# Row halves for the MLP, mixer and value products of a fused attention and MLP kernel

## The chip, the cores and the metric

The kernel runs on one core of a Trainium2 chip. The metric is the device time of one execution in microseconds (us). The time before is 290.8 us, the median of three runs (290.4 to 291.24). A ratio is the mean time of one kernel's fast runs over the mean time of the fast runs of the kernel before in the same rounds, so it is not quite the ratio of the medians that are quoted next to it.

Engine names in the profile: PE is TensorE's matmuls, PEld its weight loads, DVE is VectorE, ACT is ScalarE, POOL is GpSimd.

## The reference

Block-sparse attention over 4 batches, 8 heads, 768 positions and 64 features per head, then a low-rank mixer over the positions and an MLP with relu over the channels:

```python
scores = scale * q @ k.T                  # per head, 768 x 768
attn   = softmax(where(mask, scores, -1e9))
x      = attn @ v                         # heads side by side: [4, 768, 512]
h      = x.T @ U @ V                      # mixer, rank 32
u      = x + h.T
out    = u + maximum(u @ w_ch1, 0) @ w_ch2   # 512 -> 2048 -> 512
```

## The kernel before

The work streams by head pairs: 16 pairs, 4 per batch. The scores of a pair come in nine units. A unit is two or four matmuls into a tile `psc` of two PSUM banks, an exp of 1.02 us on ScalarE into an SBUF tile `est`, and a mask product on `est` of 0.83 us on VectorE. (In the first batch the mask comes in through further rows of the score matmuls, which use all 128 rows there, and there is no mask product.) Two `psc` tiles take four of the eight PSUM banks. The other four serve everything else: the value products (`pav`), the mixer's two products (`pa`, `ph`), MLP1 (`pt`) and MLP2 (`pch`). MLP work of the batch before is filled in between the scores of this batch, and ACT or DVE empties each bank: relu for `pt`, a sum with the residual for `ph` and `pch`, a normalisation for `pav`.

```python
    pscp = tile_pool(name="pscp", bufs=2, space=PSUM)   # two psc tiles, two banks each
    psp  = tile_pool(name="psp", bufs=1, space=PSUM)    # four tags: bank0 .. bank3
    ...
    def pst_tile(shape, dtype, name, tag=None):
        if tag is None:
            n = min(range(4), key=lambda n: banks[n])   # the bank that is free first
    ...
    def scores(i, u, est):
        psc = pscp.tile([P, 2, 512], FP32, tag="psc", name="psc")
        ...     # one head contracts over rows 0-63, the other over rows 64-127
                mm(o, kT[rows[h], kc], qT[rows[h], q0:q1], True, True)

    def weights(ests, g, j, h):                         # which unit a value matmul reads
        tr, kind = divmod(g, 2)
        if j < 4:
            return ests[3 * tr + kind][:, h, j * P : (j + 1) * P]
        return ests[3 * tr + 2][:, h, kind * QB + (j - 4) * P : ...]

    def values(i, c, ests, xs, xh):                     # c: three of six column tiles
        pav = new_pav()                                 # one bank
        for h in range(2):
            for j in range(3):
                for g in range(T):
                    mm(pav[:, j, h, :], weights(ests, g, 3 * c + j, h), vts[...], g == 0, g == T - 1)
        norm(i, c, pav, xs, xh)
    ...
        def w1(jj, c):                                  # MLP1: one bank, four full matmuls
            pt = pst_tile([P, HS], FP32, "pt")
            for cc in range(NCC):
                mm(pt, w1t[:, cc, ...], uT[:, cc, ...], cc == 0, cc == NCC - 1)
            # relu on ACT or DVE, whichever a small clock model says is done first
    ...
    groups += [stream[n : n + 2] for n in range(SINGLE, len(stream), 2)]   # scores: two units at a time
    ...
                for at, fn in zip((0, 1, 3), steps):    # values 0, values 1, product a
                    work.append((gi + at, fn))
                beside.append((gi + 5, steps[3]))       # product h, right behind scores
```

The softmax here doesn't subtract the row's maximum and nothing guards it: scores larger than these inputs give would overflow.

## Time and profile before

The first two lines of the page of the kernel before give the span and each engine's busy time, share of the span and instructions; the next two are its chain of waits, as shares of the span by engine and then by line.

```profile
span 288.9 us, 6744 instructions
PE 279.8 (97%) x2765; PEld 162.0 (56%) x2765; DVE 188.3 (65%) x347; ACT 178.0 (62%) x232; POOL 95.3 (33%) x126
...
PE 84%; DMA 6%; ACT 6%; issue 2%; DVE 1%; POOL 1%; SPq 0%; ACTq 0%; DVEq 0%; POOLq 0%
```

TensorE is busy 97 % of the time and 84 % of the chain is TensorE itself, so nothing else sets the pace. The windows view has one row per stretch: its length, then the busy time and count of PE, PEld, DVE, ACT and POOL, the granted clock, the DMA share and GB/s.

```profile
120.00:135.00 15.00, 15.00 (x182) 9.34 (x180) 11.54 (x21) 10.76 (x15) 6.26 (x8) 1.00 0.58 159
135.00:150.00 15.00, 15.00 (x138) 8.63 (x135) 12.97 (x24) 11.96 (x17) 5.18 (x7) 1.00 0.47 108
```

PE shows 15 of 15 us. The groups view, with shapes apart, names the four products that matter (busy us, mean ns of one, idle before). From the second batch on, the score matmuls and the mixer's product h use 64 rows; MLP1, MLP2, the values and the mixer's product a use 128.

```profile
L129 PE MATMUL pt<-uT,w1t 128*128 128x384 f16 x512 | 89.1, 327 | 0.2 <-DVE uT L564 0.2
L129 PE MATMUL pch<-w2t,tT 128*128 128x512 f16 x368 | 84.4, 380 | 0.0
L129 PE MATMUL pav<-vt,est 128*128 128x65 f16 x1152 | 46.4, 193 | 0.1
L129 PE MATMUL psc<-qT,kT 64*128 64x512 f16 x144 | 25.3, 382 | 0.5 <-ACT est L419 0.5
```

What the busy table does not show is TensorE's loss at changes between 64 and 128 rows, because a matmul record covers that time. It must be read from the distance between starts. An MLP1 matmul follows another after 163 ns (384 columns) and an MLP2 matmul another after 216 ns (512 columns), so 0.415 ns a column and about 3 ns. A score behind MLP1 starts after 258 ns instead of 163, behind MLP2 after 312 instead of 216, behind a value product after 126 instead of 32.

### The profile page before, as it was taken

The page shows a single profiled execution, that of the slowest core. Times are in us where ns is not written, and L with a number is a line of the kernel's source. Part 1 is how long each engine was busy: PE and PEld are TensorE (multiplying, and loading weights), DVE is VectorE, ACT ScalarE, POOL GpSimd, SP SyncE. Part 2 cuts the span into 40 slices and gives each one's busy share as a digit, 9 for nine tenths or more (in the row PEclk, how much of TensorE's full clock was granted, in tenths as well). Part 3 has the DMA queues.
Part 4 walks back from the last instruction along what each step waited for, and adds up shares of the span by engine and source line. Part 5 has one row for each costly group of instructions (what it writes and reads, how often), then busy time and mean ns, then how long its engine had stood idle before and what let it go on. Part 6 is the DMA issues. An engine that isn't in the chain of part 4 may idle for free.

```text
span 288.9 us, 6744 instructions
## 1 busy us (share of the span) xinstructions
PE 279.8 (97%) x2765; PEld 162.0 (56%) x2765; DVE 188.3 (65%) x347; ACT 178.0 (62%) x232; POOL 95.3 (33%) x126
## 2 busy tenths in 40 slices
PE   7979998899999999999999999999999999999996
PEld 2557775455746454556565545466564644665443
DVE  5756768689997978887886695779787622000112
ACT  3879999687785757577776555577875000776000
POOL 1549853207344454526244261603031201000000
PEclk9999999999999999999999999999999999999999
DMA  5999999962457677773444365161010225000122
GB/s 157 331 261 262 236 254 268 243 169 76 92 140 107 213 160 205 202 153 64 144 108 142 106 173 143 50 93 31 0 31 0 58 80 102 36 0 2 70 75 74
DMA packets 46414, 36.91 MB, mean 128 GB/s; under 512 B 27272, under 2 KB 42896, under 8 KB 46384
## 3 DMA queue, kind: packets, MB, share of 16 engines
q1 hardware_dynamic: 43208, 32.06, 41.6%
q0 software_dynamic: 2688, 4.19, 8.1%
q8 instruction: 21, 0.34, 0.5%
q10 hardware_dynamic: 488, 0.24, 0.3%
q14 instruction: 9, 0.07, 0.1%
HBM read 27.80 MB, written 6.29 MB: 118 GB/s over the span
## 4 chain that ended last, share of the span: by engine, by line
PE 84%; DMA 6%; ACT 6%; issue 2%; DVE 1%; POOL 1%; SPq 0%; ACTq 0%; DVEq 0%; POOLq 0%
PE pt L129 29%; PE pch L129 29%; PE psc L129 11%; PE pav L129 10%; ACT est L419 5%; DMA ka<-onehot_const 3%; DMA qld<-in_q_dram 2%; PE pa L129 2%; DMA kld<-in_k_dram 1%; PE ph L129 1%; PE pturn L194 0%; PE puT L563 0%; DVE uT L564 0%; DVE xh L453 0%; DVE m L384 0%
## 5 line engine op out<-in xcount | busy, mean ns | idle before, releaser
L419 ACT ACTIVATE est<-psc 128x1024 f16<-128x1024 f32 x144 | 138.8, 1023 | 47.4 <-PE psc L129 47.2
L129 PE MATMUL pt<-uT,w1t 128*128 128x384 f16 x512 | 89.1, 327 | 0.2 <-DVE uT L564 0.2
L129 PE MATMUL pch<-w2t,tT 128*128 128x512 f16 (+2 forms) x400 | 87.9, 371 | 0.0
L431 DVE TENSOR_TENSOR est<-est,m 128x1024 f16<-128x1024 f16 x108 | 84.7, 828 | 0.0
L129 PEld LDWEIGHTS <-w1t 128*128 128x128 f16 x512 | 47.6, 98 | 38.2 <-issue 8.4
L587 ACT ACTIVATE tT<-pt 128x384 f16<-128x384 f32 x82 | 39.3, 495 | 36.1 <-PE pt L129 34.9
L129 PEld LDWEIGHTS <-tT 128*128 128x128 f16 x400 | 36.4, 98 | 44.3 <-issue 5.4
L129 PEld LDWEIGHTS <-est 128*128 128x128 f16 x1152 | 44.0, 97 | 10.6 <-issue 0.5
L471 POOL CAST xh<-xs 128x384 f16<-128x384 f32 x30 | 21.4, 716 | 84.7 <-DVE xs L453 82.5
L608 DVE TENSOR_TENSOR of<-xf,pch 128x512 f32<-128x512 f32 (+2 forms) x25 | 16.6, 662 | 49.9 <-PE pch L129 49.8
L129 PE MATMUL pav<-vt,est 128*128 128x65 f16 x1152 | 46.4, 193 | 0.1
L129 PE MATMUL psc<-qT,kT 64*128 64x512 f16 (+1 forms) x288 | 33.9, 327 | 0.9 <-ACT est L419 0.8
L549 POOL CAST uh<-xf 128x384 f16<-128x384 f32 x24 | 16.1, 697 | 38.3 <-issue 33.6
L590 DVE TENSOR_SCALAR tT<-pt 128x384 f16<-128x384 f32 x46 | 24.2, 548 | 0.9 <-PE pt L129 0.7
L129 PE MATMUL psc<-qa,ka 128*128 128x512 f16 (+1 forms) x96 | 21.8, 326 | 1.9 <-DMA ka<-onehot_const 1.5
L448 DVE RECIPROCAL rcp<-pav 128x6 f32<-128x6 f32 x32 | 6.2, 194 | 21.1 <-PE pav L129 20.6
L453 DVE TENSOR_TENSOR xs<-pav,rcp 128x384 f32<-128x384 f32 x32 | 17.8, 557 | 1.9
L188 POOL CAST kst<-kld 128x768 f16<-128x768 f32 x15 | 16.5, 1100 | 5.5 <-PE pt L129 2.0
L188 POOL CAST qst<-qld 128x768 f16<-128x768 f32 x15 | 16.5, 1100 | 3.6 <-PE pa L129 2.5
L129 PEld LDWEIGHTS <-kT 64*128 64x128 f16 x288 | 10.1, 94 | 13.4 <-issue 8.8
L182 POOL CAST vt<-vld 128x768 f16<-128x768 f32 x16 | 15.0, 939 | 5.7 <-DMA vld<-in_v_dram 5.7
L544 DVE TENSOR_TENSOR xf<-xs,ph 128x384 f32<-128x384 f32 x24 | 12.2, 548 | 4.5 <-PE ph L129 4.5
(57 smaller groups left out, 111.5 us busy)
## 6 DMA issues: line engine op xcount, KB each, us to landing
vld<-in_v_dram SPq DMA_DIRECT2D x16, 384.0 KB, 5.0
out_dram<-of SPq DMA_DIRECT2D x23, 256.0 KB, 2.2
qld<-in_q_dram SPq DMA_DIRECT2D x15, 384.0 KB, 4.4
kld<-in_k_dram SPq DMA_DIRECT2D x15, 384.0 KB, 4.1
w1t<-in_moe_w_ch_dram POOLq DMA_DIRECT2D x4, 512.0 KB, 10.2
w2t<-in_moe_w_ch_dram POOLq DMA_DIRECT2D x4, 512.0 KB, 19.5
qld<-in_q_dram SPq DMA_DIRECT2D x1, 256.0 KB, 3.1
kld<-in_k_dram SPq DMA_DIRECT2D x1, 256.0 KB, 4.5
```

Source lines behind the costliest of these rows:

```text
L129: nc.tensor.matmul(out, lhsT, rhs, start=start, stop=stop, skip_group_check=loose)
L182: nc.gpsimd.tensor_copy(out=vts[b % 2][:, 2 * hp : 2 * hp + 2, :, 0:D], in_=ld)
L188: keep(nc.gpsimd.tensor_copy(out=st.rearrange("p t h d -> p h t d"), in_=ld))
L419: keep(nc.scalar.activation(out=est, in_=psc, func=AF.Exp, scale=0.125))
L431: keep(nc.vector.tensor_tensor(out=o, in0=o, in1=m, op=ALU.mult))
L453: nc.vector.tensor_tensor(out=o.rearrange("p j (h d) -> p j h d", h=2), in0=pav[:, :, :, 0:D], in1=rcp[:, :, :, None].broadcast_to([P, 3, ...
L471: keep(nc.gpsimd.tensor_copy(out=xh[:, 3 * c : 3 * c + 3, :], in_=x3))
L544: nc.vector.tensor_tensor(out=u3, in0=xs[:, tc3, :], in1=phs[c], op=ALU.add)
L549: keep(nc.gpsimd.tensor_copy(out=uh[:, tc3, :], in_=u3))
L587: keep(nc.scalar.activation(out=dst, in_=pt, func=AF.Relu))
L590: keep(nc.vector.tensor_scalar_max(out=dst, in0=pt, scalar1=0.0))
L608: nc.vector.tensor_add(out=of, in0=xfs[b][:, sc, n0:n1], in1=pchs[sc])
```

## The change

The intent is to do away with those changes of mode: the MLP, the mixer's product a and the value products also run as pairs of 64-row matmuls, one on rows 0 to 63 and one on rows 64 to 127, at the same time. The kernel keeps the two row halves out of each other's PSUM bank, so each step takes two banks. In its first phase the upper half adds into bank A and the lower half into bank B; then the halves swap, so that at the end each bank has the sum over all 128 rows. Before the swap TensorE waits on its own semaphore until the first phase is done. To hide that wait, the scores go in unit by unit between two phases, where the kernel before placed them two units at a time.

The diff, cut to its core:

```diff
+    def half_wait(ins):
+        nop = nc.tensor.nop(nofuse=True)
+        tc.add_manual_dep(nop.ins, ins.ins.name, ...)      # TensorE waits for its own matmul
 ...
-    def values(i, c, ests, xs, xh):
 ...
+    def values_rows(i, ests, xs, xh):
+        pavs = [new_pav(), new_pav()]
+        for phase in range(2):
+            if phase == 1:
+                half_wait(half_done(last))
+            for h in range(2):
+                for j in range(3):
+                    for g in range(T):
+                        for r in ((0, 1), (1, 0))[phase]:
+                            c = r ^ phase
+                            last = mm(pavs[c][:, j, h, :], weights(ests, g, 3 * c + j, h)[rows[r]], ...)
+        for c in range(2):
+            norm(i, c, pavs[c], xs, xh)
 ...
+    def mix_a_rows(xh, box):
+        pas = [pst_tile([P, P], FP32, "pa") for r in range(2)]   # summed on VectorE afterwards
 ...
+        def w1_rows(jj, phase):
+            if phase == 0:
+                pair[0] = [pst_tile([P, HS], FP32, "pt") for c in range(2)]
+            if phase == 1:
+                half_wait(pair[2])
+            for cc in range(NCC):
+                for r in ((0, 1), (1, 0))[phase]:
+                    c = r ^ phase
+                    last = mm(pts[c], w1t[rows[r], cc, ...], uT[rows[r], cc, ...], ...)
 ... (w2_rows likewise, two pch banks; the last batch's MLP stays on 128 rows)
-    groups = [[x] for x in stream[:SINGLE]]
-    groups += [stream[n : n + 2] for n in range(SINGLE, len(stream), 2)]
-    LATE = 8
+    groups = [[x] for x in stream]
+    LATE = 16
 ...
-                for at, fn in zip((0, 1, 3), steps):
-                    work.append((gi + at, fn))
-                beside.append((gi + 5, steps[3]))
+                work.append((gi, steps[0]))
+                work.append((gi + 5, steps[1]))
+                beside.append((gi + 9, steps[2]))
```

The mixer in row halves also needs another layout of its weights in the first batch: U is cast in four pieces instead of two, V is loaded twice, into two sets of rows that one cast covers, and one clearing of a tile falls away. From the second batch on, the transposes of q and k also take whichever bank is free first, where they had a fixed pair.

More of the change, by code (lines that the diff above doesn't have):

```diff
@@ L109, in pst_tile @@
             n = min(range(4), key=lambda n: banks[n])
+            assert banks[n] < OPEN
             clk["pe"] = max(clk["pe"], banks[n])
@@ L127, in mm, with half_done @@
         clk["pe"] += us
-        keep(
-            nc.tensor.matmul(
-                out, lhsT, rhs, start=start, stop=stop, skip_group_check=loose
-            )
-        )
+        ins = nc.tensor.matmul(
+            out, lhsT, rhs, start=start, stop=stop, skip_group_check=loose
+        )
+        keep(ins)
+        return ins
+    def half_done(ins):
+        return ins
+    def half_wait(ins):
+        nop = nc.tensor.nop(nofuse=True)
+        tc.add_manual_dep(
+            nop.ins, ins.ins.name,
+            mybir.DependencyInfo(mybir.DependencyClass.Sync, mybir.DependencyReason.DATA),
+            reason="halves",
+        )
+        keep(nop)
     id16 = consts.tile([P, P], FP16)
@@ L218 @@
     keep(nc.vector.memset(Vt, 0.0))
-    keep(nc.vector.memset(Vd, 0.0))
     qld, kld = new_ld(0, "q"), new_ld(0, "k")
@@ L357 @@
     uld = w2t[:, 3, 0 : 2 * T * R].bitcast(FP32)
-    mvld = w2t[0:R, 0:3, :].rearrange("r j d -> r (j d)").bitcast(FP32)
+    mvld = w2t[0 : 2 * R, 0:3, :].rearrange("r j d -> r (j d)").bitcast(FP32)
     def load_w1(cc):
@@ L480, in new_pav @@
         return pst_tile([P, 3, 2, D + 1], FP32, "pav", tag)
-    def values(i, c, ests, xs, xh):
+    def values_rows(i, ests, xs, xh):
         b, hp = divmod(i, HP)
-        pav = new_pav()
-        for h in range(2):
-            for j in range(3):
-                for g in range(T):
-                    mm(
-                        pav[:, j, h, :],
-                        weights(ests, g, 3 * c + j, h),
-                        vts[b % 2][:, 2 * hp + h, g, 0 : D + 1],
-                        g == 0, g == T - 1, us=0.0315,
-                    )
-        norm(i, c, pav, xs, xh)
+        pavs = [new_pav(), new_pav()]
[7 more added lines that the diff above has]
+                            c = r ^ phase
+                            last = mm(
+                                pavs[c][:, j, h, :],
+                                weights(ests, g, 3 * c + j, h)[rows[r]],
+                                vts[b % 2][rows[r], 2 * hp + h, g, 0 : D + 1],
+                                phase == 0 and h == 0 and j == 0 and g == 0,
+                                phase == 1 and g == T - 1, True, us=0.0157,
+                            )
+        for c in range(2):
+            norm(i, c, pavs[c], xs, xh)
     def mix_a(i, xh, box, part, tag=None):
@@ L504, in mix_a @@
             give_back(box["pa"], run_on("dve", 0.2))
+    def mix_a_rows(xh, box):
+        pas = [pst_tile([P, P], FP32, "pa") for r in range(2)]
+        for sc in range(T):
+            for r in range(2):
+                mm(pas[r], Ut[rows[r], sc, :], xh[rows[r], sc, :], sc == 0, sc == T - 1, us=0.027)
+        a16 = box["a"] = misc.tile([P, P], FP16, tag="a16", name="a16")
+        keep(nc.vector.tensor_copy(out=a16, in_=pas[0]))
+        give_back(pas[0], run_on("dve", 0.2))
+        keep(nc.vector.tensor_tensor(out=a16, in0=a16, in1=pas[1], op=ALU.add))
+        give_back(pas[1], run_on("dve", 0.2))
     def mix_h(i, c, a16, xs, uh, tag=None, quick=False):
@@ L583, in w1 @@
                 )
-            dst = tT[jj][:, c * HS : (c + 1) * HS]
-            ends = {e: max(clk[e], clk["pe"]) + d for e, d in (("act", 0.43), ("dve", 0.48))}
-            if ends["act"] <= ends["dve"]:
-                keep(nc.scalar.activation(out=dst, in_=pt, func=AF.Relu))
-                give_back(pt, run_on("act", 0.43))
-            else:
-                keep(nc.vector.tensor_scalar_max(out=dst, in0=pt, scalar1=0.0))
-                give_back(pt, run_on("dve", 0.48))
+            relu(tT[jj][:, c * HS : (c + 1) * HS], pt)
         pchs = {}
@@ L605, in w2 @@
             if part == 3:
-                of = opool.tile([P, n1 - n0], FP32, tag="of", name="of")
-                keep(
-                    nc.vector.tensor_add(out=of, in0=xfs[b][:, sc, n0:n1], in1=pchs[sc])
-                )
-                give_back(pchs[sc], run_on("dve", 0.6))
-                keep(
-                    nc.sync.dma_start(
-                        out=out[b].rearrange("(p t) d -> p t d", t=T)[:, sc, n0:n1],
-                        in_=of,
-                    )
-                )
+                leave(sc, n0, n1, pchs[sc])
@@ new lines, in mlp_steps, with relu @@
+        pair = {}
+        def relu(dst, pt):
+            ends = {e: max(clk[e], clk["pe"]) + d for e, d in (("act", 0.43), ("dve", 0.48))}
+            if ends["act"] <= ends["dve"]:
+                keep(nc.scalar.activation(out=dst, in_=pt, func=AF.Relu))
+                give_back(pt, run_on("act", 0.43))
+            else:
+                keep(nc.vector.tensor_scalar_max(out=dst, in0=pt, scalar1=0.0))
+                give_back(pt, run_on("dve", 0.48))
+        def w1_rows(jj, phase):
+            if phase == 0:
+                tT[jj] = tpool.tile([P, S], FP16, tag="tT", name="tT")
+                pair[0] = [pst_tile([P, HS], FP32, "pt") for c in range(2)]
+            uT = uTs[b].rearrange("p n t s -> p n (t s)")
+            pts = pair[0]
+            if phase == 1:
[3 more added lines that the diff above has]
+                    c = r ^ phase
+                    last = mm(
+                        pts[c],
+                        w1t[rows[r], cc, jj * P : (jj + 1) * P],
+                        uT[rows[r], cc, c * HS : (c + 1) * HS],
+                        phase == 0 and cc == 0, phase == 1 and cc == NCC - 1, True,
+                        us=0.081,
+                    )
+            if phase == 0:
+                pair[2] = half_done(last)
+            else:
+                for c in range(2):
+                    relu(tT[jj][:, c * HS : (c + 1) * HS], pts[c])
@@ new lines, in leave, with w2_rows @@
+        def leave(sc, n0, n1, pch):
+            of = opool.tile([P, n1 - n0], FP32, tag="of", name="of")
+            keep(nc.vector.tensor_add(out=of, in0=xfs[b][:, sc, n0:n1], in1=pch))
+            give_back(pch, run_on("dve", 0.6))
+            keep(
+                nc.sync.dma_start(
+                    out=out[b].rearrange("(p t) d -> p t d", t=T)[:, sc, n0:n1],
+                    in_=of,
+                )
+            )
+        def w2_rows(s0, phase, part):
+            if phase == 0 and part == 0:
+                pair[1] = [pst_tile([P, HD], FP32, "pch") for c in range(2)]
+            if phase == 1 and part == 0:
+                half_wait(pair[2])
+            for jj in range(4 * part, 4 * part + 4):
+                for r in ((0, 1), (1, 0))[phase]:
+                    c = r ^ phase
+                    last = mm(
+                        pair[1][c],
+                        tT[jj][rows[r], (s0 + c) * P : (s0 + c + 1) * P],
+                        w2t[rows[r], jj, :],
+                        phase == 0 and jj == 0, phase == 1 and jj == NJJ - 1, True,
+                        us=0.1085,
+                    )
+            if phase == 0 and part == 3:
+                pair[2] = half_done(last)
+            if phase == 1 and part == 3:
+                for c in range(2):
+                    leave(s0 + c, 0, HD, pair[1][c])
@@ new lines, in mlp_steps @@
+        if b < B - 1:
+            for jj in range(NJJ):
+                for phase in range(2):
+                    steps.append((0.65, lambda jj=jj, ph=phase: w1_rows(jj, ph), phase == 1))
+            for s0 in range(0, T, 2):
+                for phase in range(2):
+                    for part in range(4):
+                        steps.append(
+                            (
+                                0.87,
+                                lambda s0=s0, ph=phase, part=part: w2_rows(s0, ph, part),
+                                phase == 1 and part == 0,
+                            )
+                        )
+            return steps
@@ L618, in mlp_steps @@
         for jj in range(NJJ):
             for c in range(2):
-                steps.append((0.65, lambda jj=jj, c=c: w1(jj, c)))
+                steps.append((0.65, lambda jj=jj, c=c: w1(jj, c), False))
         for sc in range(T):
@@ L628, in mlp_steps @@
                             lambda sc=sc, part=part, n0=n0, n1=n1: w2(sc, part, n0, n1),
+                            False,
                         )
@@ L678, in turn_part @@
         if part == 0:
-            turning[nm] = pst_tile([P, T, P], FP16, "pturn", tag="ps")
+            turning[nm] = pst_tile([P, T, P], FP16, "pturn", tag="ps" if i < HP + 1 else None)
         turn_some(sts[i, nm], turning[nm], 3 * part, 3 * part + 3)
@@ L731, in at_unit @@
                 issue(2, "v")
-                keep(nc.sync.dma_start(out=mvld, in_=moe_V))
+                for h in range(2):
+                    keep(nc.sync.dma_start(out=mvld[h * R : h * R + R], in_=moe_V))
                 keep(
@@ L753, in at_unit @@
                 for h in range(2):
-                    keep(
-                        nc.gpsimd.tensor_copy(
-                            out=Ut[:, :, h * D : h * D + R],
-                            in_=uld.rearrange("p (t r) -> p t r", t=T),
+                    for r in range(2):
+                        at = h * D + r * R
+                        keep(
+                            nc.gpsimd.tensor_copy(
+                                out=Ut[rows[r], :, at : at + R],
+                                in_=uld[rows[r]].rearrange("p (t r) -> p t r", t=T),
+                            )
                         )
-                    )
                 keep(
                     nc.gpsimd.tensor_copy(
-                        out=Vt[0:R, :, :],
+                        out=Vt[0 : 2 * R, :, :],
                         in_=mvld.rearrange("r (p t) -> r t p", t=T),
@@ L767, in at_unit @@
             for h in range(2):
-                keep(nc.sync.dma_start(out=Vd[h * D : h * D + R], in_=Vt[0:R]))
+                keep(nc.sync.dma_start(out=Vd[rows[h]], in_=Vt[rows[0]]))
         if (i, u) in WLOADS:
@@ L799, in run_fill @@
         state["debt"] += us
+        n = 0
         while fill and state["debt"] > 0:
-            cost, fn = fill.popleft()
+            if fill[0][2] and n and us < 1e6:
+                break
+            cost, fn, _ = fill.popleft()
             fn()
+            n += 1
             state["debt"] -= cost
@@ L809, in pair_tail @@
         uh = xpool.tile([P, T, P], FP16, tag="uh", name="uh")
-        def both_a():
-            mix_a(i, xh, box, 0)
-            mix_a(i, xh, box, 1)
         def both_h():
@@ L819, in pair_tail @@
         return [
-            lambda: values(i, 0, ests, xs, xh),
-            lambda: values(i, 1, ests, xs, xh),
-            both_a,
+            lambda: values_rows(i, ests, xs, xh),
+            lambda: mix_a_rows(xh, box),
             both_h,
@@ L833 @@
         last = [n for n, gr in enumerate(groups) if (HP * b + HP - 1, NU - 1) in gr][0]
-        OPENS.append(last + 1 + LATE)
+        OPENS.append(last + LATE)
     for name in ("pe", "dve"):
@@ L901 @@
             to_come = [n for n in OPENS if n > gi] or [gi + 1]
-            run_fill(sum(c for c, _ in fill) / (to_come[0] - gi))
+            run_fill(sum(c for c, _, _ in fill) / (to_come[0] - gi))
         while work and work[0][0] <= gi:
```

## The prediction

> **What bounds it now.** TensorE. The busy table gives PE 97% of 288.9 us; the windows table gives PE 15.0 us of every 15 from 120 to 255 us, DVE at most 13, ACT at most 12. The chain of waits is 84% PE. The change touches the streaming stretch, about 49 to 230 us; the first batch and the last MLP stay.
>
> **What it removes.** Scores use 64 rows, all else 128: the build order counts 117 changes of mode after the first 64-row score, 13 after the change. The Trainium skill ("TensorEngine Tiling (Array Packing)", Key Properties) says that a change of mode drains TensorE. The trace agrees, in start-to-start times: score after MLP1 258 ns against 163 within MLP1, score after MLP2 312 against 216, score after values 126 against 32, MLP2 after a score 308 against 216; the first pair in a new mode takes 10 ns more. 104 changes at about 100 ns: -10.4 us.
>
> **What it does not gain.** Pairs of 64-row matmuls start 3 to 4 ns apart and repeat like one 128-row matmul: 109 ns at 256 columns, 56 at 128. I expect values near 32 ns a pair: after a wait ended, the sequencer passed 5 further instructions in 8 ns (47 ns for 7, 54 for 12), so issuing does not limit.
>
> **What it adds.**
> 1. 65 swap waits, each a semaphore wait in PE's sequencer. A matmul's update comes 340 ns after its start (384 columns; 207 at 65), and the one such wait of before that held PE let the next matmul start 136 ns after its semaphore, against 43 for a wait carried by a matmul. Estimate from these: a bare swap idles 312 ns (340+136-162), with a score unit in front about 100, with score and mixer none. The order shows 13 bare (12 within values) and 36 behind scores alone: 4.1+3.7 = +7.9 us.
> 2. Banks. Four banks serve MLP, values and mixer. Every step now takes two, and one pair stays half filled across a swap, so the next step must take the pair just finished. Before, an MLP1 eviction ended 0.70 us (median; 1.02 at p90) after its matmul, with three other banks. Walking one head pair through the new order with before's durations (exp 1.02, mask product 0.83, relu 0.5, norm 0.19+0.56 twice, mixer sum 0.55 twice): product a waits 0.35 us for relus, MLP1 after ph 0.65 for two sums, MLP1 after values 0.85 for two norms: about 1.6 us for each of seven head pairs in MLP1 stretches, 0.5 for five in MLP2; with some catching up, +8.5 us.
> 3. DVE gets 12 adds of 0.29 us, ACT 12 more relus: off the path.
>
> **Sum.** 290.8 - 10.4 + 7.9 + 8.5 = 296.8, so 297 us; 8 in 10 within 290 to 306. Chances: faster by over 2% 0.04, within 2% 0.46, slower by over 2% 0.50.
>
> **What would show it.** Right: no 90-ns steps between scores and MLP; pairs at 162 and 216 ns; some 65 semaphore waits on PE, bare ones with 0.31 us of idle; PE busy at 90 to 93% in the stretch, its idle time before pt, pa, pav naming DVE norms and sums and relus; clock 1.0. Step 2 is wrong if idle time before pt and pav stays under 3 us: then about 290. Step 1 is wrong if swaps clearly differ from 0.31 and 0.1 us.
>
> **What would make it wrong.** Value pairs slower than 32 ns (each 10 ns more is 8.6 us over 864 pairs); exps better spaced; relus falling where both engines are idle, so that banks come back in time.

## More of the kernel before

The view of PE's waits from 60 to 240 us has one line in all (who waits, for whom, us in total, times, longest).

```profile
PE psc L129 <- ACT est L419: 0.5, 1, 0.5
```

## The result

The changed kernel is correct and takes 315.65 us in the median (314.11 to 318.43, four runs), beside 290.6 us for the kernel before (290.26 to 291.24, four runs). The ratio is 1.087, with a 95 % interval of 1.079 to 1.096: slower, and outside the predicted range.

The page of the changed kernel, the lines that answer to those of before, and with them the row of TensorE's granted clock over 40 slices of the span:

```profile
span 316.6 us, 10037 instructions
PE 290.2 (92%) x4373; PEld 180.2 (57%) x4373; DVE 187.5 (59%) x346; ACT 184.8 (58%) x244; POOL 95.7 (30%) x128
...
PEclk9995999999999999999999999999999999999999
...
PE 59%; DVE 22%; ACT 6%; DMA 5%; issue 5%; POOL 1%; SPq 0%; DVEq 0%; ACTq 0%; POOLq 0%
```

VectorE does no more than before (187.5 us against 188.3), yet it now holds 22 % of the chain, against 1 %. The windows and groups of the changed kernel:

```profile
120.00:135.00 15.00, 13.74 (x260) 8.49 (x258) 11.57 (x20) 9.10 (x9) 6.34 (x8) 1.00 0.54 153
135.00:150.00 15.00, 12.74 (x266) 8.29 (x262) 11.16 (x20) 9.27 (x15) 4.73 (x7) 1.00 0.52 109
```

```profile
L129 PE MATMUL pt<-uT,w1t 64*128 64x384 f16 x768 | 78.2, 323 | 5.1 <-DVE of L674 2.1 <-DVE xs L467 1.4 <-DVE uT L598 0.4
L129 PE MATMUL pch<-w2t,tT 64*128 64x512 f16 x576 | 72.5, 376 | 1.6 <-DVE of L674 1.4
L129 PE MATMUL pav<-vt,est 64*128 64x65 f16 x1728 | 35.7, 190 | 7.0 <-DVE est L445 1.9 <-DVE xf L578 1.6 <-issue 1.1
```

The idle column has filled up: MLP1 waits for output sums (`of`) and normalisations (`xs`), the values for mixer sums (`xf`) and for the mask product (`est`). The view of PE's waits from 60 to 240 us, one line before, has ten now, of which seven are:

```profile
PE pt L129 <- DVE of L674: 2.1, 4, 1.3
PE pav L129 <- DVE est L445: 1.7, 8, 0.2
PE pav L129 <- DVE xf L578: 1.6, 6, 0.3
PE pa L129 <- DVE tT L645: 1.5, 2, 1.2
PE pt L129 <- DVE xs L467: 1.4, 4, 0.4
PE pav L129 <- issue: 1.1, 2, 0.6
PE pch L129 <- DVE of L674: 0.6, 2, 0.4
```

One value product of the changed kernel shows several losses at once. First TensorE, then VectorE, from the timeline (start us, busy us, count, idle before it and what ended that):

```profile
126.10 0.19 PE L129 MATMUL pav<-vt,est 64*128 64x65 f16 x1
126.56 0.49 PE L129 MATMUL pav<-vt,est 64*128 64x65 f16 x20 [0.28 <-DVE xf L578]
127.27 2.35 PE L129 MATMUL pav<-vt,est 64*128 64x65 f16 x116 [0.22 <-DVE est L445]
130.09 0.30 PE L129 MATMUL pav<-vt,est 64*128 64x65 f16 x7 [0.48 <-issue]
```

```profile
125.50 1.01 DVE L578 TENSOR_TENSOR xf<-xs,ph 128x384 f32<-128x384 f32 x2
126.43 0.79 DVE L445 TENSOR_TENSOR est<-est,m 128x1024 f16<-128x1024 f16 x1
```

The first half starts at 126.10 in a bank that is free. Its partner needs the other bank, in which the mixer's product h still lies: VectorE empties it until 126.51 us, and the partner starts at 126.56. Then the pair needs the last masked unit, whose mask product ends at 127.22; TensorE goes on at 127.27. In the third line a swap of 0.31 us (at 128.42) is hidden, because the records cover it. The fourth line starts after 0.48 us without any wait; point 7 below shows what it waited for.

### Where TensorE's time went

The records of matmuls cover a part of each such gap, so I counted from starts. For each row half, a matmul frees the array its columns times 0.415 ns, plus 2 ns, after its start; the time until the next start is idle, with a weight of one half for each row half. Gaps of a few ns, some 3 us in all in each kernel, are left out. Each idle time is put down to the semaphore that came last, as the build's list of waits tells it. The stretch runs from the first MLP1 matmul to the first matmul of the last batch's MLP, and is 194.4 us before and 216.8 us after (us, all from one profiled run each):

| | stretch | mode changes | swaps | banks | mask product | no wait found | other | idle in all |
|---|---|---|---|---|---|---|---|---|
| before | 194.4 | 10.4 | 0 | 0.9 | 0 | 0 | 2.6 | 13.9 |
| after | 216.8 | 0.3 | 9.2 | 20.1 | 3.8 | 2.9 | 1.5 | 37.8 |

"Banks" is every wait for an eviction: after the change mixer sums 5.9, output sums 5.4, relus 4.6, normalisations 3.4 and the mixer's copies and adds 0.8. The stretch less its idle time is 180.5 us before and 179.0 after. The columns to run are the same in both, so the 1.5 us between them is how closely the count closes, and the idle time accounts for the whole difference.

Outside the stretch the profiled run lost 5.3 us more, 4.5 of them before the first MLP1 matmul (54.5 against 50.0 us) and the rest behind the last output sum. In the first batch the mixer's first product waits 2.7 us for a cast on GpSimd that stands behind the new casts of U and V, and then the granted clock falls to half for 6.8 us, the 5 in the clock row. That costs 3.4 us at most, half of its length. The fastest run of the four (314.11 us) had a mean clock of 1.0, so the dip comes and goes.

### The profile page after: what moved, and what is told of

Its sections match the earlier page's. It is cut to its first block, busy times and chain, and to the rows that moved or that the text cites. A ratio compares the mean times of both kernels' runs of the same rounds, so it can differ in the third digit from the quotient of the medians.

```text
span 316.6 us, 10037 instructions
## 1 busy us (share of the span) xinstructions
PE 290.2 (92%) x4373; PEld 180.2 (57%) x4373; DVE 187.5 (59%) x346; ACT 184.8 (58%) x244; POOL 95.7 (30%) x128
## 4 chain that ended last, share of the span: by engine, by line
PE 59%; DVE 22%; ACT 6%; DMA 5%; issue 5%; POOL 1%; SPq 0%; DVEq 0%; ACTq 0%; POOLq 0%
PE pch L129 21%; PE pt L129 19%; DVE est L445 10%; PE pav L129 10%; ACT est L433 6%; PE psc L129 6%; DVE xf L578 3%; DMA kld<-in_k_dram 3%; DMA vld<-in_v_dram 3%; DVE xs L467 2%; DVE of L674 2%; PE pa L129 2%; DVE tT L645 1%; PE ph L129 1%; DVE rcp L462 1%
## 5 line engine op out<-in xcount | busy, mean ns | idle before, releaser
L129 PE MATMUL pt<-uT,w1t 64*128 64x384 f16 (+1 forms) x896 | 99.2, 324 | 5.1 <-DVE of L674 2.1
L129 PE MATMUL pch<-w2t,tT 64*128 64x512 f16 (+3 forms) x688 | 93.5, 372 | 1.6 <-DVE of L674 1.4
L129 PEld LDWEIGHTS <-w1t 64*128 64x128 f16 (+1 forms) x896 | 52.9, 94 | 42.7 <-issue 15.1
L129 PEld LDWEIGHTS <-tT 64*128 64x128 f16 (+1 forms) x688 | 43.7, 94 | 37.7 <-issue 5.1
L642 ACT ACTIVATE tT<-pt 128x384 f16<-128x384 f32 x94 | 44.9, 496 | 28.7 <-PE pt L129 27.3
L129 PE MATMUL pav<-vt,est 64*128 64x65 f16 (+1 forms) x2016 | 51.6, 191 | 7.1 <-DVE est L445 1.9
L129 PEld LDWEIGHTS <-est 64*128 64x128 f16 (+1 forms) x2016 | 46.0, 95 | 20.4 <-issue 11.0
L129 PE MATMUL psc<-qT,kT 64*128 64x512 f16 (+1 forms) x288 | 44.3, 323 | 0.3 <-ACT est L433 0.3
L129 PEld LDWEIGHTS <-kT 64*128 64x128 f16 x288 | 17.0, 94 | 8.9 <-issue 0.6
L645 DVE TENSOR_SCALAR tT<-pt 128x384 f16<-128x384 f32 x34 | 18.8, 553 | 5.2 <-PE pt L129 5.0
```

Source lines behind the costliest of these rows:

```text
L129: ins = nc.tensor.matmul(out, lhsT, rhs, start=start, stop=stop, skip_group_check=loose)
L642: keep(nc.scalar.activation(out=dst, in_=pt, func=AF.Relu))
L645: keep(nc.vector.tensor_scalar_max(out=dst, in0=pt, scalar1=0.0))
```

## The experiments

My theory: the loss is the pairs of banks. Every step holds two of four banks, a pair stays half filled across a swap, so the next step must take the pair that was just finished and wait for its evictions. In addition, values in row halves need the last masked unit at once. Rivals: the swaps cost more than they look; VectorE is loaded too heavily; the order of the scores does it; the first batch does it.

For all runs that follow, the table gives the same account of the stretch (us; "scores" is the scores' wait for exps):

| run | median us | ratio | stretch | mode | swaps | banks | mask | scores | no wait | other |
|---|---|---|---|---|---|---|---|---|---|---|
| after | 315.65 | 1.087 | 216.8 | 0.3 | 9.2 | 20.1 | 3.8 | 0 | 2.9 | 1.5 |
| e2_fuse | 311.96 | 1.075 | 213.6 | 0.4 | 4.2 | 21.1 | 3.8 | 0 | 2.6 | 2.0 |
| e7_late | 311.70 | 1.073 | 212.9 | 0.3 | 9.3 | 20.0 | 0.1 | 0 | 3.8 | 1.4 |
| e12_fuse_late | 310.37 | 1.068 | 212.2 | 0.4 | 4.6 | 22.5 | 0.1 | 0 | 4.0 | 1.9 |
| e8_three | 320.23 | 1.102 | 222.4 | 0.4 | 6.5 | 0.4 | 8.8 | 24.7 | 0.8 | 1.4 |
| e5_light_after | 308.97 | 1.064 | 210.2 | 0.2 | 9.2 | 16.7 | 0 | 0 | 3.9 | 1.3 |
| e3_values_full | 303.08 | 1.043 | 204.8 | 4.4 | 4.6 | 13.3 | 0.7 | 0 | 0.6 | 1.5 |
| e4_mlp_full | 314.15 | 1.081 | 216.1 | 20.6 | 3.9 | 1.4 | 6.4 | 0 | 1.1 | 2.6 |
| e9_mlp_only | 298.69 | 1.029 | 202.8 | 6.4 | 1.1 | 12.1 | 0.7 | 0 | 0.4 | 2.0 |
| e11_mlp1_only | 301.27 | 1.038 | 204.6 | 12.1 | 0.6 | 8.5 | 0.7 | 0 | 0.4 | 2.3 |
| e10_single_before | 300.82 | 1.037 | 204.6 | 20.7 | 0 | 1.1 | 0.4 | 0 | 0 | 2.0 |

The kernel before ran at 290.2 to 290.6 us in the same rounds. Each kernel was run in three rounds, four runs in all.

### The first batch's layout alone (e1_layout)

The kernel before with only the new layout of the mixer's weights:

```diff
-    keep(nc.vector.memset(Vd, 0.0))
-    keep(nc.sync.dma_start(out=mvld, in_=moe_V))
+    for h in range(2): keep(nc.sync.dma_start(out=mvld[h * R : h * R + R], in_=moe_V))
-    ... tensor_copy(out=Ut[:, :, h * D : h * D + R], in_=uld ...)
+    for r in range(2): ... tensor_copy(out=Ut[rows[r], :, at : at + R], in_=uld[rows[r]] ...)
```

> The kernel before with only the change's new first-batch layout (U copied in four row-half pieces, V loaded twice, no clearing of Vd), no row mode. Theory (a separate cost of about 4.4 us sits in the first batch, where product a waits 2.7 us for the xh cast behind the new copies on POOL, and a half clock may follow): 293 to 295 us, all of the loss before 32 us, the streaming stretch unchanged. Rival (all of the loss is in the streaming stretch): 290.6 us.

It took 293.41 us (292.74 to 293.68), ratio 1.009 (1.005 to 1.013), at full clock in the profiled run. The stretch is unchanged at 194.4 us; it starts 1.8 us later, and 1.1 us more pass behind the last output sum (3.6 us to the end against 2.5). Other runs with the new layout have 3.2 to 3.3 us there and those with the old one 2.5; why, I have not found out. So about 3 us of the change's 25 (1.4 to 3.8 by the interval of the ratio) come with the layout, in parts that the prediction took as "stays".

### The swap's wait on the next weight load (e2_fuse)

```diff
-        nop = nc.tensor.nop(nofuse=True)
+        nop = nc.tensor.nop()
```

With this the wait is not an instruction of its own, but is carried by the weight load behind it.

> The changed kernel with the swap wait put on the next weight load instead of a separate instruction of PE's sequencer (one word). Theory (swaps cost 9 us of the stretch by the accounting of its trace, bare 311 ns and 98 ns behind a score unit): each falls by 60 to 90 ns, swap idle 9.1 to about 5.5 us, time 312 us. Rival (swaps are the main loss, since each one empties PE's lead): 8 us or more fall away, below 308 us. If the swap is not bound by the sequencer at all: 315.6 us.

It took 311.96 us (310.89 to 314.96), ratio 1.075 (1.067 to 1.084). Swaps fell from 9.2 to 4.2 us in the account: a bare swap inside the values from 328 to 238 ns (mean of both halves), all swaps behind score units together from 5.2 to 1.3 us. The waits for banks stayed. Of 25 us, the swaps explain 9 and the form of their wait 5.

### Values one score unit later (e7_late)

```diff
-                work.append((gi, steps[0]))
+                work.append((gi + 1, steps[0]))
```

> The changed kernel with the value products one score unit later. Theory (values wait 3.8 us for the last mask product, since both column halves now run together right after it, and 3.9 us for the mixer sums that hold their banks): the mask wait falls below 0.5 us and the sums' wait by at least half, time 310 to 312 us. Rival (PE's waits only move to the next shared bank): 314 us or more.

It took 311.70 us (310.93 to 313.07), ratio 1.073 (1.068 to 1.078). The wait for the mask product fell from 3.8 to 0.1 us, as it must if its only cause is that the values come at once behind the last unit. The waits for banks changed places, mixer sums from 5.9 to 2.9 and normalisations from 3.4 to 5.3, and their sum stayed at 20.

### A third pair of banks (e8_three)

In the stretch the scores keep one two-bank tile, and the other serves MLP, mixer and values as a third pair:

```diff
+    def pst_pair(shape, name):
+        ...                                  # the oldest free pair of three
-        psc = pscp.tile([P, 2, 512], FP32, tag="psc", name="psc")
+        psc = psc_tile("psc")                # always the same one in the stretch
-            pts = [pst_tile([P, HS], FP32, "pt") for c in range(2)]
+            pts = pst_pair([P, HS], "pt")
```

> The changed kernel with three pairs of banks in the stretch instead of two: scores keep one two-bank buffer there, the other serves MLP, values and mixer. Theory (a step needs a whole pair and must take the one just finished, 20 us of waits for relus, norms, mixer sums and output sums): those waits fall to about 5 us, scores wait up to 4 us for exps, 301 to 306 us. Rival (DVE is too busy, evictions queue whatever the banks): waits stay above 15 us and 313 us or more.

It took 320.23 us (320.08 to 321.16), ratio 1.102 (1.098 to 1.107). PE's waits from 60 to 240 us in this run, all that the view lists:

```profile
PE psc L157 <- ACT est L461: 13.9, 39, 0.6
PE pav L157 <- DVE est L473: 6.1, 11, 1.0
```

None of the waits for evictions is left on the view; in the account they fall from 20.1 to 0.4 us. So it was the number of pairs: TensorE runs the very same program as in the changed kernel. One rival had to be looked at in the trace: TensorE now stalls for the scores, which in itself gives evictions more time. Where a step has an eviction to wait for, it comes 3.35 us (median) after the last matmul into that bank, against 1.72 in the changed kernel, and only some 0.4 us of the 3.35 are stalls for scores and masks. Taken off bank by bank, these stalls would bring back an estimated 0.3 us of waits. The time is no better, and not the 301 to 306 us that I expected, because the scores now wait 24.7 us for their only tile. Eight banks do not hold two pairs for the scores and three for the rest. The Trainium skill ("TensorEngine Tiling (Array Packing)", Restrictions and Gotchas, PSUM Pressure) says that row tiling increases PSUM pressure because different row tiles write to different banks. This run agrees and puts a size on it: 20 us of waits, though removing them this way costs more than they do.

### A light mask product, in both kernels (e5_light_after, e6_light_before)

Both give a wrong result: the mask product covers an eighth of its columns. In the changed kernel that takes it from 0.83 to 0.27 us and VectorE from 187.5 to 130.0 us of busy time.

```diff
-            o = est
-            m = m01[:, 2 * tr + kind, None, 0:QA].broadcast_to([P, 2, QA])
+            o = est[:, :, 0:64]
+            m = m01[:, 2 * tr + kind, None, 0:64].broadcast_to([P, 2, 64])
```

> The changed kernel with the mask product on VectorE cut to an eighth of its columns (wrong result on purpose); nothing else changes. It tells whether evictions are late because they stand behind mask products on VectorE, or because the order gives each step only the pair that was just finished. If queueing on VectorE is all: mask wait 3.8 us and nearly all of the 18 us of waits for VectorE's evictions go, about 294 us. If it is the order alone: only the mask wait goes, about 312 us. My theory: the evictions' own length (0.5 to 1.1 us for two in line) stays and about half goes, so 302 to 306 us.

> The kernel before with the same cut of the mask product (wrong result on purpose), as control for the run above. TensorE is busy throughout in it, so VectorE's load costs it next to nothing: 289.5 to 290.5 us expected by every theory. If it fell by more than 2 us, the run above would have to be read against it.

The control stayed where it was: 290.51 us (290.31 to 291.99), ratio 1.001 (0.997 to 1.005). The changed kernel took 308.97 us (307.60 to 310.86), ratio 1.064 (1.059 to 1.069), 6.7 us less. The mask wait went, and the banks fell only from 20.1 to 16.7 us, less than the half that I expected. With 31 % of VectorE's work gone, five sixths of the waits for banks remain: they are not a queue on a loaded engine. The pair is simply asked for too soon after it was finished. PE's waits from 60 to 240 us in this run, the first four of nine lines:

```profile
PE pav L129 <- issue: 1.7, 2, 1.2
PE pav L129 <- DVE xf L578: 1.5, 6, 0.3
PE pt L129 <- DVE xs L467: 1.4, 4, 0.4
PE pt L129 <- DVE of L674: 1.0, 4, 0.3
```

The lines for `xf` and `xs` are the same as in the changed kernel within 0.1 us.

### Values alone on 128 rows (e3_values_full)

```diff
-            lambda: values_rows(i, ests, xs, xh),
+            lambda: values(i, 0, ests, xs, xh),
+            lambda: values(i, 1, ests, xs, xh),
...
-                work.append((gi + 5, steps[1]))
+                work.append((gi + 2, steps[1]))
+                work.append((gi + 5, steps[2]))
```

> The changed kernel with the values alone back on 128 rows (two halves of six columns, one bank each, two score units apart); MLP and mixer stay in row halves. Bank theory: the 12 bare swaps inside the values go (3.9 us of TensorE idle), and the values no longer hold two banks at once, so the waits for norms (3.4 us) and for mixer sums in front of values (part of 5.9 us) mostly go; about 24 to 30 mode changes of 0.1 us come back (2.4 to 3 us); the wait for the last mask product (3.8 us) stays, because the first half still follows the last scores directly. Sum: 6 to 8 us off, about 308 to 310 us. Rival, that the swaps alone matter: 3.9 minus 2.7 us, so 314 us. Rival, that the row-mode values themselves are slow: 300 us or less.

It took 303.08 us (302.33 to 303.47), ratio 1.043 (1.040 to 1.046), 12.6 us less than the changed kernel and 5 us below the range that I expected. Two terms were larger than in my sum. The waits for banks fell by 6.8 us, since a value product now takes one bank and never two. The mask wait, which I expected to stay, fell to 0.7 us. The code tells why: `weights` gives the last unit (the ninth, kind 2) to column tiles 4 and 5 only, so the first half (tiles 0 to 2) does not need it. Values in row halves run all six tiles in both phases and need it at once. So about half of the change's loss is the value products.

### The MLP alone on 128 rows (e4_mlp_full), and the control for it (e10_single_before)

```diff
-        if b < B - 1:        # the MLP's row form
+        if False:
```

> The changed kernel with the MLP alone back on 128 rows; values and mixer stay in row halves. Bank theory: swaps in front of MLP1 and MLP2 (4.1 and 1.1 us) go, output sums (5.4 us) and relus (4.6 us) no longer hold up a pair of banks, nearly all mode changes come back (8 to 10 us). The values' own swaps (3.9), the mask wait (3.8) and the norms (3.4) stay. Sum: about 6 us off, 307 to 311 us. Rival, that what is lost sits in the values and the mixer: no gain, 315 us or more. Rival, that it sits in the MLP swaps: 300 us or less.

It took 314.15 us (312.93 to 315.05), ratio 1.081 (1.077 to 1.085), where I had expected 307 to 311. The waits for banks are gone (20.1 to 1.4 us), those for normalisations too, which I had expected to stay: a value product on two banks held nothing up here, with the MLP taking one bank at a time. But mode changes came back at 20.6 us and not at 8 to 10, and the wait for the mask product rose from 3.8 to 6.4. The changed kernel places scores unit by unit, and with the MLP on 128 rows each unit makes two changes. My expectation had taken the count of the order in pairs of units. To separate that order from the row halves, I ran the kernel before with its scores unit by unit and nothing else changed:

```diff
-    groups = [[x] for x in stream[:SINGLE]]
-    groups += [stream[n : n + 2] for n in range(SINGLE, len(stream), 2)]
-    LATE = 8
+    groups = [[x] for x in stream]
+    LATE = 16
-                for at, fn in zip((0, 1, 3), steps):
+                for at, fn in zip((0, 2, 5), steps):
```

> The kernel before with its scores unit by unit instead of in pairs of units, the tails at the same distance counted in units, nothing else changed: it separates the unit-by-unit order, which the change needs for its swaps, from row mode. 225 mode changes in the build order against 125, each about 0.1 us as measured, so 10 to 12 us of idle more: about 302 us (299 to 305), without bank waits. Rival, that the shorter groups alone make the bank waits: 310 us or more, with idle time before MLP1 and MLP2 that names sums and norms.

It took 300.82 us (299.78 to 301.90), ratio 1.037 (1.033 to 1.040). Mode changes cost 20.7 us in it and waits for banks 1.1, so the order alone makes no wait for banks. PE's waits from 60 to 240 us:

```profile
PE pav L129 <- DVE est L431: 0.2, 1, 0.2
```

The two orders have 107 and 208 changes in the stretch for 10.4 and 20.7 us: 97 and 99 ns each. The kernel before had already halved this cost with pairs of units, which is why so little was left for row halves to win.

### The MLP alone in row halves (e9_mlp_only), and MLP1 alone (e11_mlp1_only)

The first takes e3, brings back product a and the first batch's layout of before, and carries the swap's wait on the weight load. The second also brings back MLP2.

```diff
-            lambda: mix_a_rows(xh, box),
+            both_a,
-        nop = nc.tensor.nop(nofuse=True)
+        nop = nc.tensor.nop()
 # e11 only:
-            for s0 in range(0, T, 2): ... w2_rows(s0, ph, part)
+            for sc in range(T): ... w2(sc, part, 0, HD)
```

> Only the MLP in row halves: the values and the mixer's product a on 128 rows again, the first batch's layout as before, and the swap's wait carried by the next weight load. From the run with full values (303.1 us): swaps fall from 4.6 to about 1.3 us as in the run with carried waits, 22 more mode changes cost 2.2 us, the product a needs one bank instead of two and so waits about 1.5 us less for relus, the layout gives back about 1 us. Sum about 299 us (296 to 302). Bank theory: the waits for output sums (4.5 us) and about half of the relu waits stay, so it does not get under 292 us. Rival, that the swaps and the layout were the whole cost: 291 us or less.

> As the run with only the MLP in row halves, but MLP2 on 128 rows too, so row halves in MLP1 alone. 58 more mode changes cost about 5.8 us; the waits for output sums (4.5 us) and MLP2's swaps (0.4 us) go. About 300 us (297 to 303), one more than the run beside it. If output sums were not what held MLP2 up, it would be 5 us slower than the run beside it.

They took 298.69 us (298.55 to 298.74), ratio 1.029 (1.027 to 1.032), and 301.27 us (300.77 to 302.06), ratio 1.038 (1.036 to 1.041), each within 1.3 us of what was expected. In the first, swaps cost 1.1 us and mode changes 6.4, but waits for banks are still 12.1. Its chain of waits reads:

```profile
PE 74%; ACT 11%; DVE 11%; issue 2%; DMA 1%; ACTq 0%; DVEq 0%
```

In the second, output sums no longer hold anything up (2.8 to 0 us), and mode changes take the gain back (6.4 to 12.1). With scores unit by unit, row halves in the MLP win 2 us (298.7 against 300.8). The kernel before, on 128 rows with pairs of units, remains the fastest of all.

### Both single gains together (e12_fuse_late)

The edits of e2_fuse and e7_late in one kernel.

> The changed kernel with both single edits that helped: the swap's wait carried by the next weight load (alone 312.0 us) and the values one score unit later (alone 311.7 us), against 315.7 us. If the two costs are separate, the gains add: 308 us (306 to 309.5). Rival: the banks are then used harder and the waits for evictions grow by what the two edits give, so 310.5 us or more. Either way it stays above 298.7 us, the best with row halves in the MLP alone, because the values keep both banks of a pair.

It took 310.37 us (309.19 to 310.92), ratio 1.068 (1.064 to 1.072). The two gains, 3.7 and 4.0 us, do not add to 308: together they give 5.3 us, close to what the rival said (310.5 us or more). Waits for banks rose from 20.1 to 22.5 us. When TensorE comes to a pair earlier, it waits longer for it.

## Why the prediction was wrong

The prediction was 297 us (290 to 306), and the measured median is 315.65 us. Point by point, for the stretch:

1. Mode changes: predicted -10.4 us, measured -10.1 (10.4 to 0.3). Right. The Trainium skill ("TensorEngine Tiling (Array Packing)", Key Properties) says that changing the tiling mode drains TensorE. The traces agree at 97 to 99 ns a change in the two kernels that change most.
2. Pairs of 64-row matmuls: predicted to repeat like one full matmul, measured 165 ns (MLP1), 216 (MLP2) and 32 (values). Right. Partners start some 20 ns apart rather than the 3 to 4 ns of before, and that costs nothing.
3. Swaps: predicted +7.9 us, at 312 ns bare and about 100 behind a score unit; measured +9.2, bare ones at 311 ns in one half and 340 in the other, and some 100 ns behind a score unit. Right in mechanism and near in size.
4. Banks, "with some catching up, +8.5 us": this is the step that failed. It measured +19.2 us (0.9 to 20.1). The mechanism was the right one, as the run with a third pair shows, but the term was mis-sized. The prediction's own walk gave 1.6 us for each of seven head pairs and 0.5 for five, so 13.7 us, and then took off 5 for catching up, with nothing from the trace behind it. The runs show the opposite of catching up: with the swaps and the mask wait shortened, the waits for banks grew by 2.4 us. Even without that the walk falls 5.5 us short of what was measured. The output sums of MLP2, 5.4 us, were taken too lightly: the walk gave all of MLP2's stretches 2.5.
5. The mask product in front of the values: not in the sum at all, measured +3.8 us. The walk looked at banks and not at the weights. Row halves read all six column tiles from the start, so they need the last masked unit; the run with values one unit later took this wait away.
6. "The first batch and the last MLP stay": wrong for the first batch and a little for the end. The new layout alone costs 3.1 us (e1_layout), and one profiled run lost more to a dip of the clock.
7. Stalls without a wait: 2.9 us, not foreseen. The two large ones (0.8 and 0.6 us) come inside value products, at TensorE's matmuls 1617 and 1872. The run with the light mask, which has the same TensorE program, stalls at the same two matmuls, for 1.3 and 0.7 us, at other times. The Trainium skill ("Runtime: NRT & Kernel Launch", Instruction fetch mechanics) says that instructions are refilled in blocks of 256, mostly hidden. Here they are not always hidden, and the traces show it by place and by time. By place: counted over all TensorE instructions of the build (weight loads, matmuls, waits), thirteen stalls of 0.2 us or more in the stretch have no semaphore wait near them, in six of the kernels, and every one stands at number 194 or 195 of a block of 256. By time: the trace holds the refills, as packets of 16384 bytes on an instruction queue. Each of the thirteen stalls ends 1.4 to 2.0 us after its block's packet has landed, and at the 368 block ends of all runs that pass without a stall the packet had landed at least 1.4 us before. From the start of the packet it is 2.4 to 3.2 us, and value products in row halves run through 256 instructions in 2.05 us (64 pairs of 32 ns), while MLP1 takes 10. The prediction asked whether TensorE issues fast enough, and not whether its instructions are there. No run changes the refill alone, and about half of the 2.9 us is not placed. The instruction queue on the pages of the kernel before and of the changed one (packets, MB, share):

```profile
q8 instruction: 21, 0.34, 0.5%
q8 instruction: 34, 0.56, 0.8%
```

The sum of the stretch: -10.1 + 9.2 + 19.2 + 3.8 + 2.9, less 1.1 for other idle time, is 23.9 us more idle; less the 1.5 us by which the count does not close, 22.4 us, of which the prediction had 6.0. The banks are the largest part of the miss, 10.7 us. The stated sign that step 2 was wrong, idle before MLP1 and the values under 3 us, pointed the wrong way: I had looked for too high an estimate there and not for one too low. PE's share, 92 % of the span, fell into the band that the prediction gave for the stretch (90 to 93), so that band could not have told 297 from 316 us; the busy share hides a part of each gap.

What stays open: the smaller stalls without a wait, the cause of the dip of the clock in the first batch, and of the longer end with the new layout. The kernel before has runs with a mean clock of 0.994 too. No version was found that beats the kernel before.

## What to carry to other kernels

Before splitting a product into row halves to save mode changes, count the PSUM pairs: with two pairs, one of them open across a swap, the next step asks for the pair just finished, and each eviction (0.5 to 0.75 us for one bank here) is then in TensorE's way, even when the evicting engine has time to spare (16.7 of 20.1 us stayed with VectorE relieved). Count also what the grouping already saves: doing two score units in a row halved the mode changes (20.7 to 10.4 us) for nothing. An estimate from a walk through the order should not be reduced by a guess at overlap; look in the trace for something that could do the catching up. Row halves also double TensorE's instructions: compare how fast a stretch runs through 256 of them (2.05 us in the values here) with what a refill takes (2.4 to 3.2 us).

## What the Trainium skill lacked or had wrong

- "TensorEngine Tiling (Array Packing)", Key Properties: gives no figure for the drain at a change of mode. These runs show 97 to 99 ns a change, the same in two kernels with 107 and 208 changes.
- The same page, PSUM Pressure: says that row tiles need different banks, but not what it takes to let both halves add into one result. Here it took a wait of TensorE for its own matmul: 328 ns bare inside value products as an instruction of its own, 238 ns carried by the next weight load; for all swaps behind a score unit 5.2 us as an instruction and 1.3 us carried. No page has these costs.
- The same page has no word on how many pairs of banks row halves need in all so that evictions stay out of the way. Here two pairs lost 20.1 us to evictions, three pairs 0.4.
- "TensorE: Matmul & The Clock Gate", Packing small matmuls, The mechanism: says that matmuls start strictly in program order. In the changed kernel the two row halves drift apart, and an MLP2 matmul that follows all six `ph` matmuls in the program starts before the last three of them (timeline of the changed kernel):

```profile
124.60 0.33 PE L129 MATMUL ph<-a,Vd 64*128 64x128 f16 x3
124.76 0.38 PE L129 MATMUL pch<-w2t,tT 64*128 64x512 f16 x1
124.79 0.33 PE L129 MATMUL ph<-a,Vd 64*128 64x128 f16 x3
```

- "Runtime: NRT & Kernel Launch", Instruction fetch mechanics: says that refills are mostly hidden. In six kernels with value products in row halves, thirteen stalls of 0.2 to 1.3 us without any wait stand at the ends of blocks of 256 instructions, and each ends 1.4 to 2.0 us after the block's packet has landed.
